# First feed-forward layer of the last two chunks in seven half products, with the weight sums on VectorE and GpSimd

## The chip, the cores and the metric

One core of a Trainium2 chip. The metric is the device time of one execution in microseconds (us). Times are medians of several executions. An execution over 1.5% above the fastest of its kernel is counted as slow (353.23 us in j_early_gaps, whose fastest is 347.66); all ratios here use fast executions alone, and only the medians of after_again and j_early_gaps contain one slow execution each (without it 352.01 and 349.17 us). TensorE (matmul), VectorE, ScalarE and GpSimd run side by side here (busy for 97%, 79%, 62% and 55% of the same 348.5 us in the kernel before); the profile calls them PE, DVE, ACT and POOL. In these kernels the matmuls write PSUM tiles ("ps" in the views), and the other tiles are in SBUF. The granted clock is the share of its full clock that the trace shows for TensorE.

## The reference

An attention block (B = 8, heads = 8, S = 576, D = 64) makes x, and a gated feed-forward network follows.

```python
# pooled attention (4:1) repeated, plus attention in a band of |i - j| < 4  ->  x: 4608 x 512
gate = np.maximum(x @ w_gate, 0.0)      # w_gate: 512 x 1536
val  = x @ w_val                        # w_val:  512 x 1536
out  = (gate * val) @ w_out             # w_out: 1536 x 512, fp32
```

The kernel computes in fp16 with fp32 accumulation. Of the attention only one thing matters here: it ends at about 275 us of 350, and its tiles (V buffers "vw", query and key buffers "qk", the transposed x "xT") then come free for other use.

## The kernel before

Tokens are processed in nine chunks of 512 (0 to 8). The first layer of a chunk is 12 column groups ("ff" groups) of gate and value, each four matmuls of 512 columns. The second layer already works in seven half products: a 2x2 product of blocks in seven multiplications rather than eight, at the price of sums of the operands and of the results. The line numbers of the profile are noted.

```python
def emit_h_mm(c, jj, pp, which, kks):           # first layer, plain; matmul is L588
    w = (wg_sb, wv_sb)[which]
    for kk in kks:
        nc.tensor.matmul(out=pair(pp)[:, which, :], lhsT=w[:, kk, bass.ts(jj, 128)],
                         rhs=xT[:, kk, c * TCH : (c + 1) * TCH],
                         start=(kk == 0), stop=(kk == 3))

def emit_relu(pp):                              # ScalarE, PSUM -> SBUF
    ...
def emit_gate(c, jj, pp, r1):                   # L609, VectorE
    nc.vector.tensor_tensor(out=gT[c % 2][:, jj, :], in0=r1, in1=pair(pp)[:, 1, :], op=ALU.mult)

class Unit:                                     # second layer, seven half products
    def sums(self, lo=0, hi=NK, which=range(4)):        # L678, VectorE, SBUF + SBUF
        (a11, a12), (a21, a22) = self.x
        ops = ((self.s1, a21, a22, ALU.add), (self.s2, self.s1, a11, ALU.subtract),
               (self.s3, a11, a21, ALU.subtract), (self.s4, a12, self.s2, ALU.subtract))
        ...
    def mm(self, out, left, right, first): ...          # L684, six matmuls of 256 columns
    def p1(self): self.mm(self.a, self.x[0][0], half_js[0][0], True)
    ...                                                 # p2 .. p7
    def keep(self, i): nc.scalar.copy(...)              # L718, ScalarE
    def c11(self): nc.vector.tensor_tensor(...)         # L721, VectorE, PSUM + SBUF

def emit_tail_slot(s, gate): ...                # chunks 7 and 8: plain first layer between products

# the attention's sum of its two parts; VectorE, two SBUF operands, one read with stride 0
def emit_xsum(hp):                              # L504
    nc.vector.tensor_tensor(out=xT[...], in0=xn[...], in1=_sap(x, (0, 128), 288, [..., [0, 4]]), op=ALU.add)
```

The softmax here doesn't subtract the row's maximum and nothing guards it: scores larger than these inputs give would overflow.

## Time and profile before

| | before |
|---|---|
| time, median of the first 3 runs | 350.16 us (349.41 to 350.61) |
| span of the profiled execution | 348.5 us, granted clock 0.998 |
| TensorE, VectorE, GpSimd busy | 97%, 79%, 55% |
| VectorE busy from 275 to 345 us | 37.66 of 70 us |
| tail: from the last two gates of chunk 6 to the end | 72.46 us |

The last row is how the end of the kernel is compared here. What comes before about 275 us varies by up to some 4 us between executions, so spans are not taken one from another. In every trace VectorE does the last two gates of chunk 6 as a pair, at 273 to 277 us where nothing was held up before (288.5 and 281.6 us in the two runs where it was); the **tail** is the span less the start of that pair. In this line of VectorE's timeline (start, duration, engine, line, operation, operands, count) it is at 276.00:

```profile
276.00 1.28 DVE L609 TENSOR_TENSOR gT<-r,ps 128x512 f16<-128x512 f16 x2
...
278.31 0.22 DVE L678 TENSOR_TENSOR vw<-gT 128x128 f16<-128x128 f16 x1
```

348.5 - 276.00 = 72.5. The second line, one of the sums of the second layer, is noted for later: it takes 0.22 us here.

### The profile page before, as it was taken

To read this page: it belongs to the slowest core of one execution; us is meant where nothing else is said; L and a number is where in the kernel's file an instruction comes from. 1 tells how busy PE (TensorE), PEld (TensorE's weight loads), DVE (VectorE), ACT (ScalarE), POOL (GpSimd) and SP (SyncE) were. 2 spreads that over 40 slices of the span, in tenths; PEclk is the share of its full clock that TensorE was granted. 3 is DMA by queue.
4 is the path that set the end of the run, shared out by engine and by line. 5 is a ranking of instruction groups with operands and counts; after the bars stand their busy time and mean duration, and the time that the engine had idled before them with its cause. 6 is when DMAs were issued, how large, how long until landed. Compare 5 with 4: busy or idle time off the path is not lost. (4 is left out here: it accounts for less than half of the span.)

```text
span 348.5 us, 7968 instructions
## 1 busy us (share of the span) xinstructions
PE 339.4 (97%) x3127; PEld 204.6 (59%) x3127; DVE 277.0 (79%) x479; ACT 214.5 (62%) x390; POOL 191.3 (55%) x233
## 2 busy tenths in 40 slices
PE   6899999999999999999999999999999999999996
PEld 2665555545475756565666556665666555655575
DVE  4895567788899999999999999999989755354481
ACT  3767776677666776677667767676777443333332
POOL 8976656999999994998298949830300000000000
PEclk9999999999999999999999999999999999999999
DMA  9999999999999999999999999951101001001013
GB/s 145 164 172 186 186 190 162 162 174 181 165 139 193 127 159 117 128 172 136 112 118 169 155 101 109 171 120 20 61 3 60 2 32 45 30 32 45 18 45 120
DMA packets 168772, 40.29 MB, mean 116 GB/s; under 512 B 150080, under 2 KB 165664, under 8 KB 168736
## 3 DMA queue, kind: packets, MB, share of 16 engines
q0 software_dynamic: 132960, 22.93, 88.4%
q1 hardware_dynamic: 35056, 15.79, 24.3%
q10 hardware_dynamic: 720, 1.08, 0.9%
q8 instruction: 24, 0.39, 0.5%
q14 instruction: 12, 0.10, 0.1%
HBM read 46.45 MB, written 9.44 MB: 160 GB/s over the span
## 5 line engine op out<-in xcount | busy, mean ns | idle before, releaser
L588 PE MATMUL ps<-xT,wv_sb 128*128 128x512 f16 x432 | 109.6, 379 | 0.5 <-DVE gT L609 0.4
L588 PE MATMUL ps<-xT,wg_sb 128*128 128x512 f16 x432 | 110.0, 380 | 0.1
L609 DVE TENSOR_TENSOR gT<-r,ps 128x512 f16<-128x512 f16 x108 | 72.8, 681 | 37.7 <-PE ps L588 30.3
L605 ACT ACTIVATE r<-ps 128x512 f16<-128x512 f32 x108 | 64.2, 595 | 49.6 <-PE ps L588 48.9
L588 PEld LDWEIGHTS <-wv_sb 128*128 128x128 f16 x432 | 41.0, 98 | 47.1 <-issue 1.1
L588 PEld LDWEIGHTS <-wg_sb 128*128 128x128 f16 x432 | 39.8, 98 | 36.9 <-DVE xT L581 0.6
L545 DVE TENSOR_TENSOR xn<-ps,rden 64x720 f16<-64x720 f32 x46 | 41.6, 905 | 5.1 <-ACT rden L541 4.0
L536 ACT ACTIVATE rden<-ps 64x720 f32<-64x720 f32 x46 | 35.2, 764 | 16.1 <-PE ps L526 15.2
L376 ACT ACTIVATE ee<-ps 112x576 f16<-112x576 f32 x64 | 38.2, 647 | 10.5 <-PE ps L366 9.3
L327 POOL TENSOR_TENSOR vd<-v 72x256 f16<-72x256 f32 x23 | 20.1, 884 | 32.1 <-PE ps L526 31.6
L233 POOL DMA_DIRECT2D qk<-in_q_dram x46 | 33.8, 740 | 6.1 <-DMA wo_sb<-in_moe_w_out_dram 2.8
L382 DVE TENSOR_TENSOR ee<-ee,cst_sb 112x576 f16<-112x576 f16 x64 | 33.9, 549 | 3.0 <-ACT ee L376 2.0
L233 POOL DMA_DIRECT2D qk<-in_k_dram x46 | 33.8, 739 | 1.4 <-DMA qk<-in_k_dram 0.6
L684 PEld LDWEIGHTS <-gT 128*128 128x128 f16 x288 | 28.2, 98 | 10.3
L258 POOL DMA_DIRECT2D vw<-in_v_dram x30 | 28.7, 956 | 7.3 <-DMA wo_sb<-in_moe_w_out_dram 1.9
L275 DVE TENSOR_REDUCE qkd<-qkT 128x288 f16<-128x1152 f16 x23 | 30.9, 1342 | 0.9 <-DMA qkT<-qk 0.9
L321 POOL TENSOR_TENSOR v<-v 72x512 f32<-72x512 f16 x23 | 30.1, 1309 | 1.3 <-DMA v<-in_v_dram 0.8
L718 ACT COPY q<-ps 128x256 f32<-128x256 f32 x39 | 14.5, 371 | 20.4 <-PE ps L684 20.1
L684 PEld LDWEIGHTS <-xo 128*128 128x128 f16 x240 | 22.7, 98 | 5.9
L684 PE MATMUL ps<-wo_sb,gT 128*128 128x256 f16 x192 | 24.9, 273 | 0.0
L504 DVE TENSOR_TENSOR xT<-xn 128x576 f16<-128x576 f16 x28 | 22.7, 810 | 0.6
L518 PE MATMUL ps<-ee,vw 112*128 112x96 f16 x276 | 20.5, 205 | 0.7 <-DVE ee L382 0.5
(103 smaller groups left out, 475.5 us busy)
## 6 DMA issues: line engine op xcount, KB each, us to landing
out_dram<-y_sb SPq DMA_DIRECT2D x20, 256.0 KB, 3.4
vw<-in_v_dram POOLq DMA_DIRECT2D x30, 168.0 KB, 6.2
qk<-in_q_dram POOLq DMA_DIRECT2D x46, 72.0 KB, 5.6
qk<-in_k_dram POOLq DMA_DIRECT2D x46, 72.0 KB, 5.8
v<-in_v_dram POOLq DMA_DIRECT2D x23, 144.0 KB, 5.8
out_dram<-y_sb SPq DMA_DIRECT2D x22, 128.0 KB, 1.7
wg_sb<-in_moe_w_gate_dram POOLq DMA_DIRECT2D x4, 384.0 KB, 10.2
wv_sb<-in_moe_w_val_dram POOLq DMA_DIRECT2D x4, 384.0 KB, 10.6
```

Source lines behind the costliest of these rows:

```text
L233: nc.gpsimd.dma_start(dst.rearrange("p (j h d) -> p j h d", h=2, d=64)[:, :, hh, :], _dap(src, off + hh * S * D, [[D, 96], [NQ * D, NB], [ ...
L258: nc.gpsimd.dma_start(t, _dap(v, base, [[D, WK], [NQ * D, n], [1, D]]))
L275: nc.vector.tensor_reduce(out=qkd[hp % 2].rearrange("p i t -> p (i t)"), in_=qkT[hp % 4][:, 0 : 2 * S].rearrange("p (t f) -> p t f", f=4), ...
L321: nc.gpsimd.tensor_tensor(out=m, in0=t[:, :, 0:128], in1=t[:, :, 128:256], op=ALU.add)
L376: nc.scalar.activation(out=o, in_=ps[0:WK, p0 + 2 * g : p0 + 2 * g + 2, 0:288], func=AF.Exp, scale=scale)
L382: nc.vector.tensor_tensor(out=o, in0=o, in1=_sap(masks_sb, (0, WK), 288 * g, [[0, 2], [1, 288]]), op=ALU.mult,)
L536: nc.scalar.activation(out=rden[lo : lo + 64], in_=ps[de : de + 64, 4 + 2 * hh : 6 + 2 * hh, 0:360], func=AF.Ln)
L545: nc.vector.tensor_tensor(out=xn[lo : lo + 64], in0=ps[lo : lo + 64, 4 + 2 * hh : 6 + 2 * hh, 0:360], in1=rden[lo : lo + 64], op=ALU.mult,)
L588: nc.tensor.matmul(out=pair(pp)[:, which, :], lhsT=w[:, kk, bass.ts(jj, 128)], rhs=xT[:, kk, c * TCH : (c + 1) * TCH], start=(kk == 0), st ...
L605: nc.scalar.activation(out=r1, in_=pair(pp)[:, 0, :], func=AF.Relu)
L609: nc.vector.tensor_tensor(out=gT[c % 2][:, jj, :], in0=r1, in1=pair(pp)[:, 1, :], op=ALU.mult)
L684: nc.tensor.matmul(out=out, lhsT=left[:, i, :], rhs=right[i], start=(first and i == 0), stop=(i == NK - 1), skip_group_check=True,)
```

## The change

The intent: do the gate groups 2 to 5 of chunk 7 with their partners 8 to 11, and all gate and value groups of chunk 8, by seven half products too. A pair (j, j+6) of one matrix then takes 14 matmuls of 256 columns rather than 8 of 512. There are 16 such "blocks". They need four sums of each weight matrix, four sums of x for each chunk, copies and sums of the products. The gate's weight sums ("wg") are on VectorE, the value's ("wv") on GpSimd, in 16 instructions. The first value sum goes into the V buffer of pair 31, the last pair of the attention, so GpSimd's sums wait until that pair's products are done. The order of all steps of the tail is a hand-written list.

```diff
+TAIL = """
+wv/00/ p/1/60 gate/4 hg/0/71 wv/01/ gate/5 hg/0/70 wg/0/ hv/1/70 relu/0/70 sumhi/0/60 xs/0/7
+relu/0/71 hg/1/70 sumhi/1/60 wg/2/ hg/1/71 relu/1/70 wg/1/ keep/1/60 qg/1/72 qg/2/72 keepg/1/72
+hv/0/70 xs/1/7 xs/2/7 gate/1/70 wv/20/ qg/1/73 qg/6/72 p/2/60 keepg/2/72 next/0 wv/21/ next/1
# ... 37 more lines of steps
+"""
-    def emit_tail_slot(s, gate):
# ... removed: plain first layer of chunks 7 and 8
+    ws = [qkfull[0:4],
+          [vwfull[3].rearrange(...)] + qkfull[4:7]]                # weight sums: gate, value
+    def emit_ws(w, i, lo, hi, eng):                                # L902 of the new kernel
+        g = (wg_sb, wv_sb)[w]
+        # s1 = a21+a22, s2 = s1-a11, s3 = a11-a21, s4 = a12-s2
+        eng.tensor_tensor(out=o, in0=a, in1=b, op=op)
+    def emit_xs(c, i):                                             # L911, VectorE
+        nc.vector.tensor_tensor(out=o, in0=a, in1=b, op=ALU.subtract)
+    class Block:
+        def q(self, i):                                            # L936, 2 matmuls of 256 columns
+            x, s = xs[c - NCH + 2], ws[self.w]
# ...       the seven products
+        def keep(self, i):
+            nc.scalar.copy(out=self.m[i], in_=self.a)
+        def out(self, arg):                                        # L952 ScalarE, L955 VectorE
# ...
+    def emit_tail_step(kind, arg, at):
# ...
+        elif kind in ("gateg", "gateb"):                           # L976: max(h, 0) * value
+            nc.vector.scalar_tensor_tensor(..., op0=ALU.max, op1=ALU.mult)
+        elif kind == "wg":
+            emit_ws(0, i, 0, 768, nc.vector)                       # 128x1536 each
+        elif kind == "wv":
+            emit_ws(1, i, 192 * int(arg[1]), 192 * int(arg[1]) + 192, nc.gpsimd)   # 128x384 each
# ...
-        last = [tail_unit(NCH - 1, u, b) for u, b in ((0, (4, 5, 6)), (1, (7, 2, 3)))]
# ... removed: the old loop over the tail's slots
+        for tok in TAIL.split():
+            ...
```

In the list "qg/1/72" is product 1 of the gate block 2 of chunk 7, "xs/1/7" the second sum of x of chunk 7, "sumhi/0/60" part of a sum for unit 0 of chunk 6.

## The prediction

> **What bounds the kernel now.** I read the busy shares first, then the forty slices, the chain that ended last, the groups of the last 72 us, and the timeline of the end.

> ```profile
> PE 339.4 (97%) x3127; PEld 204.6 (59%) x3127; DVE 277.0 (79%) x479; ACT 214.5 (62%) x390; POOL 191.3 (55%) x233
> ...
> PE   6899999999999999999999999999999999999996
> ...
> DVE  4895567788899999999999999999989755354481
> ...
> POOL 8976656999999994998298949830300000000000
> ...
> PE 19%; DVE 0%; issue 0%
> PE ps L588 12%; PE ps L684 8%; DVE gT L609 0%; DVE y_sb L725 0%
> ```

> TensorE is full in all slices but the first and last. VectorE, nearly full in the middle, falls to a half in the last ten slices, and GpSimd has nothing to do there. The chain is TensorE alone: the last 68 us are first-layer products (L588) and second-layer half products (L684) back to back. So here a matmul less is time less, as long as nobody makes TensorE wait. That is what the change bets on.

> ```profile
> 276.08 0.81 PE L588 MATMUL ps<-xT,wg_sb 128*128 128x512 f16 x3
> 277.33 0.81 PE L588 MATMUL ps<-xT,wv_sb 128*128 128x512 f16 x3 [0.45 <-DVE gT L609]
> ...
> 332.84 0.42 DVE L678 TENSOR_TENSOR vw<-gT 128x512 f16<-128x512 f16 x1
> 333.17 0.42 DVE L678 TENSOR_TENSOR vw<-gT,vw 128x512 f16<-128x512 f16 x1
> ...
> 338.68 0.42 DVE L721 TENSOR_TENSOR y_sb<-ps,q 128x256 f32<-128x256 f32 x1
> 339.01 0.41 DVE L721 TENSOR_TENSOR y_sb<-ps,v 128x256 f32<-128x256 f32 x1
> ```

> The timeline shows the one wait of TensorE in the tail (0.45 us), and that two VectorE instructions that wait for nothing start 0.33 us apart though each is shown as 0.42: about 0.09 us of each overlaps the next.

> ```profile
> L382 DVE TENSOR_TENSOR ee<-ee,cst_sb x64: 443/457/1404, 10.2 to 269.0; 112x576 f16<-112x576 f16 x64
> ...
> L504 DVE TENSOR_TENSOR xT<-xn x28: 740/757/1606, 36.9 to 275.2; 128x576 f16<-128x576 f16 x28
> ...
> L321 POOL TENSOR_TENSOR v<-v x23: 1142/1178/2369, 68.9 to 245.7; 72x512 f32<-72x512 f16 x23
> L327 POOL TENSOR_TENSOR vd<-v x23: 712/746/1329, 70.1 to 246.9; 72x256 f16<-72x256 f32 x23
> ```

> These are minimum, median and maximum of VectorE and GpSimd work on two SBUF operands. The minimum is that work alone; the maxima, two to three times as long, are where the two engines meet.

> [...]eight 512-wide matmuls take 1.73 us in the chain (216 each), six 256-wide ones 0.66 (109 each). The mean times that the profile's groups give for one (379 and 273 ns) hold the pipeline too and are not used. [...]128x512 takes 419 ns from SBUF in f16 and 685 with one operand in PSUM; 128x256 from PSUM takes 420. [...]here (1142 - 712) / 256 = 1.7 ns[...].

> **The change part by part.** TensorE. A plain pair (j, j+6) of one matrix costs 2 x 4 matmuls of 512 columns = 1.73 us. A block has seven products of 2 matmuls of 256 columns = 14 x 0.1092 = 1.53. It saves 0.20 us[...]. Chunk 7 has gate blocks for pairs 2 to 5 (4), chunk 8 gate and value blocks for pairs 0 to 5 (12): 16 x 0.197 = 3.2 us. The second layer is unchanged at 42 half products. Counting the new list from its first half product: 16 plain first-layer groups 13.8 + 112 block products 24.4 + 42 half products 27.5 = 65.7 us. Before, the same stretch is 16 + 32 plain groups of 0.863 and the 42 half products, 68.9, plus the 0.45 wait: 69.4, and the trace has 69.6 (275.4 to 345.0). The new order puts a half product and other banks first, so that wait may go too. With no new wait: 350.16 - 3.2 - 0.4 = 346.6 us. That is the floor.

> ScalarE. Per block three copies of 128x256 that keep sums and one output copy, 0.372 each: 64 x 0.372 = 23.8, plus 24 such for the six units 8.9 and 4 relus 2.4: 35 us in 66. It has room.

> VectorE, by the durations of like rows: 48 block outputs x 0.42 = 20.2; 26 gates x 0.69 = 17.9 (the 20 new ones do max and multiply in one instruction; [...]taken as the old gate's 0.685); 18 unit outputs 7.6; sums of gT, whole and in parts, 16.0; sums of x 8 x 0.42 = 3.4; gate weight sums 4 x 0.95 (the 128x1536 row, 952 ns alone) = 3.8. That is 68.9 us in 146 instructions, against 65.7 of TensorE; before, VectorE was busy about 38 us in the same stretch. Overlap takes 0.09 off each that follows directly, at most 13 us, so real occupation is some 57 to 60 of 66: from half to nearly nine tenths. That is the price.

> By stage, from the list's order (TensorE / VectorE by durations / its count): until the first product of unit 1 of chunk 6, 13.2 / 13.1 / 23; until the first value block, 14.1 / 15.1 / 29; value blocks, 27.9 / 30.0 / 63; after the last block, 10.5 / 10.6 / 31.

> GpSimd. 16 value weight sums of 384 elements: 0.3 us fixed + 384 x 1.68 ns = 0.93 us, 15 us in all. The first writes the V buffer of pair 31, whose last reader is the L518 group of that pair, ended near 271.2 in the trace. So they run from 271 to 287 undisturbed[...]. The first value block comes 27.6 us of TensorE work into the list, 303 or later, and needs them one product later. The buffer's hold does not reach the end; it only puts these sums beside the 14 or so two-SBUF sums of VectorE of that time.

> **Where waits come back.** First 13 us: VectorE has 13.1 - 2 of work, begins 0.6 us late (gate at 276.0, list at 275.4), and meets GpSimd. Single meetings cost it 0.25 to 0.85 us (the L504 maximum less its median); with half of 14 hit at 0.4 that is 3 us. It ends 1 to 2 us behind, and TensorE needs its weight and x sums early: I put 1.0 us. Middle 42 us: an eviction hand-off is 0.27 - 0.11 of matmul tail + 0.37 + some 0.05 at each end, 0.6 us, four in a block, so 0.9 + 2.4 = 3.3 us for a block's chain. The single value slot takes six blocks in 27.9 us, 4.7 each: enough, but with VectorE at nearly nine tenths in strict order some waits slip through: 0.6. End: last block's tail 0.2, output 0.42, gate 0.69 = 1.3 us, for which two half products (1.31) are in store; then the last sums come just after the products that want them: 0.6 us, against none before. Sum 2.2 us, as an estimate. 346.6 + 2.2 = **348.8 us**, that I predict.

> **Rivals.** (1) VectorE becomes the bound. For: 68.8 us by durations in a 66 us stretch, and fp32 gates whose one-instruction form this trace never shows; if they cost 1.0 us rather than 0.69, 6 us come on top. Against: the measured overlap. It would give 351 to 356. (2) The GpSimd sums are late or block VectorE throughout: if each of 14 meetings costs 0.8 us, VectorE loses 11 us in the first 25, of which TensorE might wait 5: about 352. Against: most L504 and L382 instructions pass GpSimd untouched. (3) Nothing returns: the list fits and the full saving shows, 346.6. For: before, TensorE waited 0.45 us in 70. (4) The eviction chain through ScalarE sets the pace: 16 chains x 3.3 us in three slots is 18 us in 50, so no.

> **Range and chances.** No path leads to 2% faster (343.2): the floor is 346.6, and 3.6 us is 1% of the time. 2% slower (357.2) needs 11 us of waits, rival 1 and 2 together. The range is the floor up to a third of rival 1: 346.6 to 351.2. Faster 0.01, same 0.96, slower 0.03.

> **What would show it.** TensorE has 128 fewer matmuls of 512 columns and 224 more of 256. VectorE's last ten slices go from 4-5 to 8-9. GpSimd is idle from 248 to about 271 and done before 295. New gates average near 0.69 us. Waits of TensorE after 275 add up to 1 to 4 us, most of them ended by VectorE, some at the start and some after the last block. I am wrong if TensorE waits over 6 us there, if value blocks wait for GpSimd, or if the gates are far from 0.69.

## The result, and the profile after

| | before | after |
|---|---|---|
| median (range, runs) | 349.99 (349.41 to 350.61, 4) | 353.12 (352.53 to 353.76, 4) |
| tail in the profile | 72.46 | 75.25 |
| waits of TensorE in the tail | 0.45 | 3.49 |
| VectorE busy, 275 to 345 us | 37.66 | 64.31 |

The ratio of after to before is 1.009 (95% interval 1.0064 to 1.0115). All ratios here are the mean time of one kernel's fast runs over that of the other's of the same rounds, so they are not quite the ratios of the medians. The kernel is 3 us slower; 348.8 had been predicted, and the range ended at 351.2.

The page of the new kernel, the busy shares and four rows of the slices (a digit is the busy share of a fortieth of the span in tenths; PEclk is TensorE's granted clock in tenths):

```profile
PE 338.9 (96%) x3223; PEld 215.2 (61%) x3223; DVE 306.1 (87%) x547; ACT 223.8 (64%) x434; POOL 209.1 (60%) x249
...
PE   6999999999999999999999999999999969999996
...
DVE  5895667798899999999999999999987997999994
...
POOL 8986656899999895979497959721101980000000
PEclk9999999999999999999999999999999979999999
```

VectorE's last slices went from 4 and 5 to 9, as expected, and TensorE is nevertheless full there. Only slice 33 stands out, in two rows: TensorE at 6 and its clock at 7. GpSimd has a block of work beside it. So the loss sits in one spot, around 282 to 291 us. All that TensorE waited for from 270 us on is one line (waited for: in total, times, longest):

```profile
PE ps L936 <- DVE xT L911: 3.5, 1, 3.5
```

It is the first product with a sum of x. In TensorE's timeline the wait ends at 285.45, and two matmuls of 256 columns are shown at 0.61 us rather than the 0.38 just before it:

```profile
281.58 0.38 PE L936 MATMUL ps<-xT,wg_sb 128*128 128x256 f16 x2
285.45 0.61 PE L936 MATMUL ps<-xT,qk 128*128 128x256 f16 x2 [3.49 <-DVE xT L911]
```

The reason is in the windows (stretch, length, then busy time and count of PE, PEld, DVE, ACT and POOL, granted clock, DMA share, GB/s):

```profile
284.60:285.45 0.85, 0.00 (x0) 0.00 (x1) 0.85 (x2) 0.00 (x0) 0.85 (x2) 0.52 0.00 0
285.45:291.46 6.01, 6.01 (x23) 3.40 (x24) 5.98 (x10) 1.04 (x3) 2.88 (x3) 0.50 0.06 22
291.46:300.00 8.54, 8.54 (x66) 6.33 (x65) 6.32 (x15) 3.34 (x11) 0.00 (x0) 1.00 0.10 33
```

From 284.6 to 291.5 TensorE's clock was halved. So 6.01 us of work ran at half speed, a loss of 3.0. The wait was 3.49 us, and the half clock lasted 6.83 us. It began inside the wait: the clock fell at 284.60, 2.64 us after the end of the last matmul before the wait (281.96). What the runs together show of this is under "The clock alone".

Now VectorE, which TensorE waited for:

```profile
275.96 1.29 DVE L651 TENSOR_TENSOR gT<-r,ps 128x512 f16<-128x512 f16 x2
277.16 1.22 DVE L902 TENSOR_TENSOR qk<-wg_sb 128x1536 f16<-128x1536 f16 x1
278.31 0.93 DVE L720 TENSOR_TENSOR vw<-gT 128x128 f16<-128x128 f16 x1
279.16 1.15 DVE L911 TENSOR_TENSOR xT<-xT 128x512 f16<-128x512 f16 x1
280.23 0.93 DVE L720 TENSOR_TENSOR vw<-vw,gT 128x128 f16<-128x128 f16 x1
281.08 1.68 DVE L902 TENSOR_TENSOR qk<-wg_sb 128x1536 f16<-128x1536 f16 x1
282.69 1.66 DVE L902 TENSOR_TENSOR qk<-qk,wg_sb 128x1536 f16<-128x1536 f16 x1
284.27 2.17 DVE L911 TENSOR_TENSOR xT<-xT 128x512 f16<-128x512 f16 x2
...
290.66 0.95 DVE L902 TENSOR_TENSOR qk<-wg_sb,qk 128x1536 f16<-128x1536 f16 x1
```

A sum of 128x128 takes 0.93 us where the same form took 0.22 before; a sum of 128x1536 takes 1.22 to 1.68, and 0.95 once GpSimd is done (last line). GpSimd's 16 sums run from 270.93 to 288.3, and every one of the eight VectorE sums of two SBUF operands from 277.16 on runs beside them. The first and the last lines of GpSimd there:

```profile
270.93 1.78 POOL L902 TENSOR_TENSOR vw<-wv_sb 128x384 f16<-128x384 f16 x2 [23.38 <-PE ps L560]
...
283.49 4.83 POOL L902 TENSOR_TENSOR qk<-wv_sb,qk 128x384 f16<-128x384 f16 x4
```

GpSimd's own sums take 0.9 us each at the start of that stretch and about 1.2 at its end. The two gates at 275.96 are a control within the same trace: one of their operands is in PSUM, GpSimd is busy beside them, and they take 1.29 us against 1.28 in the kernel before.

**A ledger of the tail.** Before: 72.46. Less the old wait, 0.45, and the saving of 16 blocks, 3.2: 68.8. Plus the wait of 3.49 and the half clock of 3.0: 75.3. The trace has 75.25.

### The profile page after: what moved, and what is told of

It reads as the page before. It is cut to its first block, busy times and chain, and to the rows that moved or that the text cites. A ratio compares the mean times of both kernels' runs of the same rounds, so it can differ in the third digit from the quotient of the medians.

```text
span 351.2 us, 8305 instructions
## 1 busy us (share of the span) xinstructions
PE 338.9 (96%) x3223; PEld 215.2 (61%) x3223; DVE 306.1 (87%) x547; ACT 223.8 (64%) x434; POOL 209.1 (60%) x249
## 3 DMA queue, kind: packets, MB, share of 16 engines
q1 hardware_dynamic: 35056, 15.79, 23.8%
## 4 chain that ended last, share of the span: by engine, by line
PE 87%; DVE 7%; ACT 2%; DMA 2%; issue 1%; DVEq 0%; POOLq 0%
PE ps L630 43%; PE ps L726 20%; PE ps L936 7%; PE ps L560 3%; PE ps L660 3%; PE ps L397 2%; PE ps L408 2%; PE ps L336 2%; PE ps L568 2%; DMA qk<-in_k_dram 2%; DVE xn L587 1%; DVE xo L720 1%; DVE qk L902 1%; DVE xo L482 1%; DVE gT L651 1%
## 5 line engine op out<-in xcount | busy, mean ns | idle before, releaser
L630 PE MATMUL ps<-xT,wv_sb 128*128 128x512 f16 x384 | 98.5, 383 | 0.0
L630 PE MATMUL ps<-xT,wg_sb 128*128 128x512 f16 x352 | 89.0, 380 | 0.1
L647 ACT ACTIVATE r<-ps 128x512 f16<-128x512 f32 x88 | 52.2, 595 | 28.3 <-PE ps L630 28.1
L651 DVE TENSOR_TENSOR gT<-r,ps 128x512 f16<-128x512 f16 x88 | 59.2, 681 | 12.4 <-ACT r L647 6.3
L630 PEld LDWEIGHTS <-wv_sb 128*128 128x128 f16 x384 | 36.7, 99 | 39.2 <-issue 1.3
L630 PEld LDWEIGHTS <-wg_sb 128*128 128x128 f16 x352 | 32.0, 98 | 32.3 <-DVE xT L623 0.6
L418 ACT ACTIVATE ee<-ps 112x576 f16<-112x576 f32 x64 | 38.3, 649 | 10.5 <-PE ps L408 9.3
L578 ACT ACTIVATE rden<-ps 64x720 f32<-64x720 f32 x46 | 35.2, 766 | 15.0 <-PE ps L568 14.1
L424 DVE TENSOR_TENSOR ee<-ee,cst_sb 112x576 f16<-112x576 f16 x64 | 30.9, 507 | 2.7 <-ACT ee L418 2.0
L946 ACT COPY vw<-ps 128x256 f32<-128x256 f32 x48 | 16.7, 375 | 19.9 <-PE ps L936 14.7
L546 DVE TENSOR_TENSOR xT<-xn 128x576 f16<-128x576 f16 x28 | 25.1, 895 | 0.6
## 6 DMA issues: line engine op xcount, KB each, us to landing
wv_sb<-in_moe_w_val_dram POOLq DMA_DIRECT2D x4, 384.0 KB, 10.6
```

The lines of the kernel that those rows point to most:

```text
L418: nc.scalar.activation(out=o, in_=ps[0:WK, p0 + 2 * g : p0 + 2 * g + 2, 0:288], func=AF.Exp, scale=scale)
L424: nc.vector.tensor_tensor(out=o, in0=o, in1=_sap(masks_sb, (0, WK), 288 * g, [[0, 2], [1, 288]]), op=ALU.mult,)
L578: nc.scalar.activation(out=rden[lo : lo + 64], in_=ps[de : de + 64, 4 + 2 * hh : 6 + 2 * hh, 0:360], func=AF.Ln)
L630: nc.tensor.matmul(out=pair(pp)[:, which, :] if out is None else out, lhsT=w[:, kk, bass.ts(jj, 128)], rhs=xT[:, kk, c * TCH : (c + 1) * TCH],
L647: nc.scalar.activation(out=r1, in_=pair(pp)[:, 0, :] if h1 is None else h1, func=AF.Relu)
```

## The experiments

**Theory T1, contention:** GpSimd's value sums, running beside VectorE's sums of two SBUF operands, stretch the first stage of the tail; TensorE waits for a sum of x, and a wait that long (3.49 us) brings the half clock. **Theory T2, VectorE is full:** the new work of VectorE, in strict order, is what TensorE waits for, with GpSimd or without. A third question is how much the hold of the sums by the V buffer has to do with it. The table has all runs; they are read below one by one. Where an experiment shortens the list of steps, the line numbers in its profile are smaller by some 40 for the same statements.

| run | correct | median us (runs) | ratio to before [95%] | tail | TensorE waits in the tail |
|---|---|---|---|---|---|
| a_no_pool_sums | no, on purpose | 346.79 (6) | 0.9895 [0.9856, 0.9934] | 68.75 | none |
| b_early_buffer | yes | 358.81 (6) | 1.0231 [1.0189, 1.0273] | 68.74 | none (9.5 before it) |
| c_warm | yes | 351.20 (6) | 1.0014 [0.9976, 1.0051] | 73.64 | 0.7 + 0.6 + 0.4 |
| f_dve_order | yes | 353.16 (6) | 1.0086 [1.0046, 1.0127] | 75.3 | 0.2 + 0.7 + 3.6 |
| after_again | yes | 352.19 (15) | 1.0055 [1.0029, 1.0081] | 74.69 | 3.5 + 0.6 |
| d_pool_later | yes | 349.82 (14) | 0.9997 [0.9971, 1.0023] | 71.52 | 1.7 + 0.6 |
| g_vector_sums | yes | 347.49 (9) | 0.9931 [0.9904, 0.9958] | 69.41 | none |
| j_early_gaps | yes | 349.27 (22) | 0.9972 [0.9951, 0.9994] | 68.75 | none (2.0 before it) |
| l_pool_memsets | no, on purpose | 347.46 (8) | 0.9907 [0.9868, 0.9946] | 68.74 | none |
| k_gaps | yes | 355.07 (6) | 1.0102 [1.0047, 1.0157] | 73.68 | 1.2 + 0.7 (3.0 before it) |

Each ratio is against runs of the kernel before on the same chip; kernels of one series (the first four, the next four, the last two) share those. A tail is of one execution, which was the fastest of its kernel in c, d, g, j and l and the slowest in k. The medians bear the tails out: where TensorE was not held up before the tail, each lies within 0.7 us of 346.79 plus what its tail is longer than 68.75.

### Without GpSimd's sums

```diff
-            x, s = xs[c - NCH + 2], ws[self.w]
+            x, s = xs[c - NCH + 2], ws[0]          # value blocks use the gate's sums: wrong result
...
         elif kind == "wv":
-            emit_ws(1, i, 192 * int(arg[1]), 192 * int(arg[1]) + 192, nc.gpsimd)
+            pass
```

> The change with GpSimd's 16 sums left out; the value blocks read the gate sums in their place, so the result is wrong on purpose, and nothing else differs. Theory 1 ([...]the early VectorE sums come late, TensorE waits 3.5 us and then runs 6.8 us at half clock): VectorE's first sums fall back to their short times (128x1536 near 0.95 us, 128x512 near 0.42), no wait of TensorE above 1 us after 275, no half clock, 346.5 to 347.5 us. Theory 2 (VectorE simply has too much work in the last 70 us, GpSimd or not): TensorE still waits 3 us or more around 282 and the time stays above 350.

The result is wrong (relative error 0.66), as intended; the work of TensorE and VectorE is the same as in the changed kernel. TensorE waits for nothing from 240 us on, and the tail is 68.75 us, where the ledger without waits says 68.8. The median falls to 346.79. T2 does not stand against this: VectorE does all that it does in the changed kernel, and nobody waits for it. But GpSimd idle and GpSimd not reading are not told apart by this run; see the memsets below.

### The sums in a buffer that is free earlier

```diff
-        for rs in ((4, 5), (6, 0))
+        for rs in ((3, 5), (6, 0))
...
-        [vwfull[3].rearrange("p b c -> p (b c)").rearrange("p (i c) -> p i c", i=2)] + qkfull[4:7],
+        [vwfull[4].rearrange("p b c -> p (b c)").rearrange("p (i c) -> p i c", i=2)] + qkfull[4:7],
```

> The change with the first value sum in the buffer of pair 25's V in place of pair 31's (the two buffers swap their uses), so that the buffer no longer holds GpSimd. Its sums should start near 247.7, when its attention work ends, and end near 265 to 268. Theory 1: the early VectorE sums of the tail meet nobody, the wait at 282 and the half clock go; what the meetings cost in 248 to 268 instead (VectorE is at nine tenths there) decides between 347 (absorbed) and 350 (TensorE waits there). Theory 2: above 350, with the wait at 282 still there.

The tail is as good as without the sums, 68.74 us, and yet this is the slowest version, 358.81. The timeline shows why: VectorE's instruction that ends the attention of a pair, GpSimd's sums beside it, and TensorE.

```profile
249.65 12.05 DVE L546 TENSOR_TENSOR xT<-xn 128x576 f16<-128x576 f16 x1
...
253.26 3.50 POOL L902 TENSOR_TENSOR qk<-vw,wv_sb 128x384 f16<-128x384 f16 x4
...
257.59 3.50 POOL L902 TENSOR_TENSOR qk<-wv_sb,qk 128x384 f16<-128x384 f16 x4
...
262.69 0.40 PE L560 MATMUL ps<-ee,vw 112*128 112x96 f16 x3 [9.51 <-DVE ee L424]
```

A VectorE instruction that takes 0.74 us at its shortest in this trace (median 0.76) stands here for 12.05. It ends at 261.7, 0.6 us after GpSimd's last sum (261.1). GpSimd's sums run on at 0.87 us each as if nothing were beside them. TensorE then waits 9.5 us, with half clock for 13.65 us. So the hold by the buffer decides where the contention falls, and not whether. Without it the attention is hit, where it cost more: the expectation had allowed 350 us at most for this.

### The clock alone

```diff
-hv/0/70 xs/1/7 xs/2/7 gate/1/70 wv/20/ qg/1/73 qg/6/72 p/2/60 ...
+hv/0/70 xs/1/7 xs/2/7 gate/1/70 wv/20/ qg/1/73 warm/26/ qg/6/72 p/2/60 ...
+            if kind == "warm":      # 26 matmuls of zeros, 256 columns, into a bank not in use
```

> The change with 26 idle matmuls of 256 columns (2.8 us, result unused) put into TensorE's queue where it waits 3.5 us, so that the array isn't idle for the whole wait. If the half clock that follows the wait is caused by the idleness, it does not occur (granted clock near 1.00 in 285 to 292), and the time falls by about 3 us, to 350 us, the wait itself remaining. If the clock falls for another reason, or if the idle matmuls delay the work, the time stays at 353 or rises.

This fills the wait with matmuls whose results nobody uses. They keep TensorE active until shortly before the sum of x is there:

```profile
279.21 3.00 PE L1169 MATMUL ps<-zero_sb 128*128 128x256 f16 x26
282.87 0.39 PE L936 MATMUL ps<-xT,qk 128*128 128x256 f16 x2 [0.66 <-DVE xT L911]
```

The clock stays at 1.00 over the whole tail, and the tail falls from 75.25 to 73.64; against the repeat of the changed kernel, 74.69, the gain is 1.0. The tail adds up without a half clock: 68.75, 3.0 of useless matmuls and 1.7 of waits are 73.45, against 73.64. So the half clock is a cost of its own, beside the wait, and here it comes from TensorE having nothing to do: with the 26 matmuls in the wait the clock is 1.00, in the first profile without them 0.50. The gain is a third to a half of the 3 us that were expected, because the useless matmuls and the waits beside them (4.7 us) took 1.2 us more than the one wait of 3.49. In the times alone the gain is clear against the first runs of the changed kernel (1.0014 against 1.009), not against the repeat (1.0055), whose interval overlaps.

### Another order on VectorE

```diff
-... relu/0/70 sumhi/0/60 xs/0/7 relu/0/71 hg/1/70 sumhi/1/60 wg/2/ ... hv/0/70 xs/1/7 xs/2/7 gate/1/70 wv/20/ ...
+... relu/0/70 xs/0/7 relu/0/71 hg/1/70 ... hv/0/70 xs/1/7 gate/1/70 wg/2/ xs/2/7 wv/20/ ... keepg/2/72 sumhi/0/60 sumhi/1/60 next/0 ...
```

> The change with four VectorE instructions moved back in its queue: the two short gT sums, the third gate weight sum and the third x sum now come after the four sums that the first s2 product needs; GpSimd as it was. Theory 1: that product's operands are ready some 3.5 us sooner, the wait at 282 falls below 1 us and the half clock goes; but VectorE still loses the same time to GpSimd by 292, so other TensorE waits of together 1 to 3 us appear: 348 to 350 us. Theory 2, or if the wait is on something else than these sums: no gain.

The four sums that the waiting product does not need come later. The wait at 282 us goes from 3.49 to 0.17, and a new one takes its place 7 us on:

```profile
282.43 0.39 PE L897 MATMUL ps<-xT,qk 128*128 128x256 f16 x2 [0.17 <-DVE xT L872]
...
289.03 0.92 PE L687 MATMUL ps<-wt,vw 128*128 128x256 f16 x6 [3.57 <-DVE vw L681]
```

The tail is 75.3 as before, with 3.41 us of half clock after the new wait; the 348 to 350 us expected did not come. This is what lost capacity looks like: VectorE lacks the time of the first stage, and the order only chooses who waits for it. The run alone would also fit T2; together with the first run it does not.

### The changed kernel once more

No edit: a second set of runs, for the series that follows.

> The changed kernel itself once more, as the reference for the runs sent with it: about 353 us, 3 us over the kernel before, with the wait of some 3.5 us near 282 and a stretch of half clock after it.

The median was 352.19, the ratio 1.0055; both intervals, this and 1.0064 to 1.0115, lie above 1. The wait is again 3.5 us, plus one of 0.6, but the half clock now covers only one step of 3.413 us and costs 1.7. The ledger 68.75 + 3.5 + 0.6 + 1.7 gives 74.55; the trace has 74.69. So part of the loss differs from run to run: 6.83 us of half clock after the wait of 3.49 in the first profile, 3.41 after one of 3.5 here. The contention itself does not: the eight VectorE sums take the same times as in the first profile to 0.01 us.

### GpSimd's sums a few us later

```diff
-wv/00/ p/1/60 gate/4 hg/0/71 wv/01/ ...          # wv steps spread over the list
+... hv/0/70 xs/1/7 xs/2/7 wv/00/ wv/01/ wv/20/ ... wv/33/ gate/1/70 ...
...
+            if arg == "00":                        # makes the first sum wait for xs/2/7
+                x3 = xs[0][2][:, :, 0:16]
+                nc.gpsimd.tensor_tensor(out=ws[1][0][:, :, 0:16], in0=x3, in1=x3, op=ALU.add)
```

> The change with GpSimd's sums held longer: the first of them now also needs the third x sum of chunk 7, so they begin after the four early VectorE sums, near 281, and end near 299; the value blocks need them from 304. If what costs is only where the two engines meet (the early sums), the wait at 282 goes and 347 to 349 us come out. If the total of the meetings counts, because VectorE has nearly no slack anywhere in 281 to 300 either, waits of 2 us or more return later, and it stays at 350 to 354.

The 16 sums run from 279.7 to 296.3 us. The early VectorE sums are at their short times, the contention falls on later ones, and 1.7 us is the longest wait:

```profile
PE ps L897 <- DVE xT L916: 1.7, 1, 1.7
```

The clock stays at 1.00 and the tail is 71.52. The ratio, 0.9997, is 0.006 lower than that of the changed kernel in the same series. The same sums on the same engine, begun 5.6 us after the pair of gates rather than 5.0 before it, give back 2 us of time. The result falls between the two expectations: 3.2 of the 5.9 us by which the tail of the repeat was over 68.75 went with the place of the meetings, and most of the rest stayed as waits of 2.3 us.

### The value's sums on VectorE

```diff
+        elif kind == "vv":
+            emit_ws(1, i, 0, 768, nc.vector)       # in the list after sum/3/60, keepg/1/74 and xs/3/8
...
+                if (tok, c) == ("gate/3/1", c1 - 1):
+                    emit_ws(1, 2, 0, 768, nc.vector)     # this sum before a gate of chunk 6
# all wv steps removed from the list
```

> The value sums on VectorE, as four instructions of 128x1536 at about 0.95 us, put where the run without GpSimd sums had VectorE idle (one near 272, the others near 287, 291 and 301); GpSimd does nothing in the tail, the result is right. Theory 1[...]: VectorE can do the 3.8 us itself more cheaply than it can share with GpSimd: no wait above 1 us, no half clock, 347 to 348.5 us, faster than both kernels. Theory 2 (VectorE is full): the extra 3.8 us show in TensorE's waits, 350 us or more.

This gives VectorE four more instructions of 128x1536, so it is the hardest test of T2. They take 0.95 us each. VectorE is busy for 59.18 us of 63, TensorE for 62.81, and TensorE shows no wait from 200 us on:

```profile
275.00:338.00 63.00, 62.81 (x512) 49.80 (x510) 59.18 (x144) 30.94 (x90) 0.00 (x0) 1.00 0.12 39
```

```profile
284.32 0.95 DVE L863 TENSOR_TENSOR vw<-wv_sb 128x1536 f16<-128x1536 f16 x1
```

The result is correct, the median 347.49 and the ratio 0.9931. It is the fastest correct version, ahead of both kernels. T2 falls as the cause of the loss: at 94% busy by durations VectorE holds TensorE up by 0.7 us, as long as GpSimd reads nothing beside it. That is the 0.66 us by which the tail, 69.41, is longer than without any value sums. Set beside a_no_pool_sums matmul by matmul, three start later: at 289.46, 290.95 and 299.41, by 0.30, 0.19 and 0.20 us. Each starts within 0.06 us of the end of a VectorE instruction; the first and the last of these follow directly on an added sum (287.86 and 298.07). The list of waits shows none of the three, since it counts from the modelled end of the matmul before.

### Early sums with gaps between them

```diff
# the edit of b_early_buffer, and
             emit_ws(1, i, 192 * int(arg[1]), 192 * int(arg[1]) + 192, nc.gpsimd)
+            nc.gpsimd.memset(v4[0][:, 0, 0:128], 0.0)
```

> The run with the early buffer, in which one VectorE sum stood 12 us while 13 GpSimd sums followed each other without a gap, with a short GpSimd memset (72x128, no SBUF input) after each sum. If VectorE is let in wherever GpSimd reads nothing for a moment, no VectorE sum stands longer than one GpSimd sum (about 1 us above its own time), TensorE's 9.5 us wait goes, and 347 to 351 us come out. If VectorE must wait for the whole run of GpSimd work whatever it is, the 12 us and 358 us stay.

The early placement had left VectorE standing over many GpSimd instructions, and my explanation was that GpSimd's sums follow each other without a gap. Here a write of 0.20 us stands between them. VectorE's sums from 248 to 263 us take 1.3 us at most rather than one of 12, TensorE waits 2.0 us in all, and the time falls from 358.81 to 349.27. That fits the explanation. It is not shown by it, as the next series tells.

### Writes rather than reads on GpSimd

```diff
# the first edit of a_no_pool_sums, and
         elif kind == "wv":
-            emit_ws(1, i, 192 * int(arg[1]), 192 * int(arg[1]) + 192, nc.gpsimd)
+            nc.gpsimd.memset(ws[1][i][:, :, 0:400], 0.0)
```

> As the run without GpSimd sums (value blocks read the gate sums, wrong on purpose), but GpSimd does 16 memsets of 128x800 into the same buffers at the same place, held in the same way; a memset reads nothing. If what delays VectorE is that both engines read SBUF operands, VectorE's early sums keep their short times beside the memsets and the tail from chunk 6's last gate to the end stays near 68.8 us, 346.5 to 347.5 us in all. If any work of GpSimd delays VectorE, its sums take about twice as long again and the time goes back to 351 to 353 us.

GpSimd writes at the place of the sums, from 269.58 to 282.0 us, and reads nothing. VectorE:

```profile
275.59 0.95 DVE L902 TENSOR_TENSOR qk<-wg_sb 128x1536 f16<-128x1536 f16 x1
276.46 0.22 DVE L720 TENSOR_TENSOR vw<-gT 128x128 f16<-128x128 f16 x1
276.59 0.42 DVE L911 TENSOR_TENSOR xT<-xT 128x512 f16<-128x512 f16 x1
276.93 0.22 DVE L720 TENSOR_TENSOR vw<-vw,gT 128x128 f16<-128x128 f16 x1
277.06 0.95 DVE L902 TENSOR_TENSOR qk<-wg_sb 128x1536 f16<-128x1536 f16 x1
277.93 0.95 DVE L902 TENSOR_TENSOR qk<-qk,wg_sb 128x1536 f16<-128x1536 f16 x1
278.80 0.75 DVE L911 TENSOR_TENSOR xT<-xT 128x512 f16<-128x512 f16 x2
```

All eight sums are at their time alone, though GpSimd is busy beside each. The tail is 68.74. So it is not GpSimd's activity as such that delays VectorE: the eight sums take 4.55 us beside 16 instructions that only write, against 9.8 beside the 16 that read. One reservation: the writes take 12 us in all, the sums about 17.

### The changed kernel with gaps

```diff
             emit_ws(1, i, 192 * int(arg[1]), 192 * int(arg[1]) + 192, nc.gpsimd)
+            nc.gpsimd.memset(v4[0][:, 0, 0:128], 0.0)
```

> The change with a short GpSimd memset after each of its sums, as in the run with the early buffer and gaps, but with the sums where the change has them. In the changed kernel's trace VectorE already got in after each GpSimd sum, so if a meeting costs one GpSimd sum, the gaps alter little: the wait near 282 stays between 2.5 and 4 us and the time between 351 and 353.5 us. If VectorE's delay there too comes from GpSimd following itself without a gap, the wait falls below 1.5 us and the time below 350.

This was to test the explanation with the gaps. The result, 355.07 us, lies above both expectations, and the trace refutes the explanation:

```profile
277.00 4.61 DVE L546 TENSOR_TENSOR xT<-xn 128x576 f16<-128x576 f16 x1
```

```profile
277.75 0.20 POOL L990 MEMSET v<- 72x128 f16 x1
277.92 0.91 POOL L902 TENSOR_TENSOR vw<-wv_sb 128x384 f16<-128x384 f16 x1
278.77 0.20 POOL L990 MEMSET v<- 72x128 f16 x1
```

The sum that ends the attention stood for 4.61 us, across several of GpSimd's sums and the gaps between them. TensorE waited 3.0 us for it, ahead of the tail, and 1.9 in the tail. Two steps of half clock followed. The ratio is 1.0102, no better than without the gaps. (The profiled execution is the slowest of the six, 357.11.) In the changed kernel itself the same instruction took 0.85 us beside GpSimd's sums, and in j_early_gaps 1.23. Why it takes 4.61 us in one run and 0.85 or 1.23 in others stays **open**. The two runs in which it stood are not told from the other two by gaps.

## Why the prediction was wrong

The direction was wrong: 1.4 us faster was predicted, 3 us slower measured. Step by step:

- **The floor was right.** Without waits 346.6 us was the figure; the run without GpSimd's sums has a median of 346.79, and its tail of 68.75 is the 72.46 - 3.2 - 0.45 that the count of matmuls gives. The bound was read correctly too: TensorE, and a matmul less is time less.
- **The prices were right.** The new gates are at 0.69 (minimum, median, maximum in ns):

```profile
L976 DVE SCALAR_TENSOR_TENSOR gT<-xT x12: 681/686/692, 315.4 to 338.6; 128x512 f16<-128x512 f32 x12
```

- **GpSimd's place was right.** "So they run from 271 to 287 undisturbed", and "done before 295": 270.93 to 288.3. No value block waited for them.
- **The step that failed** is "First 13 us", in two terms. The first is the size of the meeting of the two engines: "with half of 14 hit at 0.4 that is 3 us. It ends 1 to 2 us behind, and TensorE needs its weight and x sums early: I put 1.0 us." The eight sums from 277.16 to 286.4 were all hit. They take 1.22 + 0.93 + 1.15 + 0.93 + 1.68 + 1.66 + 1.12 + 1.12 = 9.8 us (the pair of 2.17 counted as two with their overlap), against 4.55 beside the memsets: 5.3 us more, 0.66 for each on average. I had taken the median of rows where most instructions meet no GpSimd sum at all (in the kernel before 17 of the 28 of L504). Beside GpSimd back to back, nine of eleven VectorE instructions with two SBUF operands lost 0.27 us or more; the other two, at 275.08 and 286.96, lost 0.1. TensorE's wait was 3.5 us, not 1.0.
- **The second term was missing**, and it is the larger error: no row of the sum allows for the half clock that followed this wait. It cost 3.0 us in the first profile and 1.7 in the repeat. All waits together were 3.49 us, within the "1 to 4 us" that the prediction gave and 1.3 over its 2.2; the other 3.0 of the 4.3 us between 348.8 and 353.12 are the half clock. Without it the time would have been about 350.1, an estimate from these numbers, and inside the range.
- **Two terms were too dark**, which hid part of the error. "some waits slip through: 0.6" in the middle and "0.6 us" at the end: with GpSimd quiet the list of waits was empty in three runs. With these at 0, the sum is 346.6 + 3.5 + 3.0 = 353.1. That it meets the median of 353.12 so closely is partly luck, since the half clock differs from run to run; for the repeat it gives 346.6 + 4.1 + 1.7 = 352.4, against 352.19.
- **A reading was wrong without harm.** "(1142 - 712) / 256 = 1.7 ns" sets a row that reads f16 (72x512) against one that reads f32 (72x256), so it is not the price of 256 more elements of one kind. The 0.93 us that came of it was near the 0.87 at which undisturbed sums followed each other. And of the four maxima "where the two engines meet", three stand beside a sum of the other engine; the 1404 of L382, at 89.69 us, has only GpSimd's DMA issues beside it.
- **Rival 1**, VectorE as the bound, is refuted (a, l, and g above all). **Rival 2** named the mechanism: it said 0.8 us for each meeting, a TensorE wait of 5 and about 352 us. Measured were 0.66, 3.5 and 353.12. That the time came so near is partly luck, since the rival had no half clock either and too long a wait in its place. What was held against it, "most L504 and L382 instructions pass GpSimd untouched", is the same misreading as in the failed step.
- **The hold by the buffer** was thought harmless: "only puts these sums beside the 14 or so two-SBUF sums of VectorE of that time". That is right as a mechanism, and it put the harm where TensorE felt it. Earlier is worse without gaps (1.0231), a little later is better (0.9997), and off GpSimd is best (0.9931).

Shown: the loss is GpSimd's reads beside VectorE's sums of two SBUF operands on a stretch where TensorE needs VectorE soon, plus the half clock that followed the wait (3.0 us in the first profile). Open: what decides how long a VectorE instruction stands beside GpSimd's reads.

## What to carry to other kernels

Before moving sums to an idle engine, look at what the other engines read from SBUF at that time. With GpSimd's sums back to back, nine of the eleven VectorE instructions with two SBUF operands beside them were hit here, mostly by about 0.7 us, and in another run one by 11 us; so look at what TensorE needs from VectorE at that moment. Compare the price of the same work on the busy engine: four instructions of 0.95 us on a VectorE at 94% were cheaper than sixteen on a GpSimd with nothing to do (347.49 against 352.19 us in the same series). And a TensorE wait should be counted with the half clock that may follow it: here it followed the waits of 3.0 us and more and cost up to 3.0 us in all after a wait of 3.5; waits of 1.7 us and less brought it once, as a pair in one step.
